# Spreading a closed expert's eight penalties over ScalarE's queue, and starting the first expert on halves of 256 columns

## The chip, the cores and the metric

One core of one Trainium2 chip runs the whole program. The metric is the device time of one execution in microseconds (us); several executions give a median. The engines are TensorE (PE in the rows; PEld is its loading of weights), VectorE (DVE), ScalarE (ACT), GpSimd (POOL) and SyncE (SP). Each takes the instructions of its own queue in the order in which the program put them there.

## The reference

The input is filtered by an FFT along its sequence, and the result goes through eight experts, each with a fixed capacity. Which token goes to which expert is settled by a greedy walk over all scores, highest first:

```python
y = np.fft.irfft(np.fft.rfft(x, axis=1) * F, n=x.shape[1], axis=1)   # 8 x 2496 x 256
x = y.reshape(19968, 256); cap = 19968 // 8                          # 2496 tokens each
logits = x @ w_gate
for idx in np.argsort(-logits.flatten()):
    tok, e = idx // 8, idx % 8
    if assigned[tok] >= 0 or counts[e] >= cap: continue
    assigned[tok] = e; counts[e] += 1
for e in range(8):
    m = assigned == e
    out[m] = np.maximum(x[m] @ w1[e], 0.0) @ w2[e]                   # w1 256x1024, w2 1024x256
```

## The kernel before

**Stages.** The class `Fft` computes the filter and the scores `lg`, and stores the filtered rows to the DRAM tensor `xs`. The class `Route` finds the experts in the order in which they fill up: phase `ph` finds the expert that closes next, its threshold and its members. The class `Ffn` runs that expert. The FFT's last stores of `xs`, the routing of expert 0 and the load of its weights meet at one place, called the handover here.

**One expert.** `Ffn.gather` fetches tokens from `xs` by an index list `xid`, 128 to a tile `xg`, one indirect DMA on POOL's queue each. The 2496 tokens make five groups `g` of 512 (the last of 448), each of four tiles. `Ffn.turn(e, g, h)` turns half a group, two tiles, on PE (`ptr`), then ACT copies it as the rounded high part into a tile named `xo`, and DVE writes the rest into a tile named `z` (the names are those of older tiles whose space is used again). A block `f` of the first product is six matmuls `pz<-xo,w0h`, `pz<-z,w0h`, `pz<-xo,w0l`, three for each half of the 256 inputs, over the 512 columns of a group; eight blocks make the 1024 hidden values. ACT's relu copy (`hl<-pz`, L867) and a DVE instruction (L869) then write the block's high and low part. The second product (`py`, L904) sums 24 matmuls of 256 columns, ACT copies its result (`y`) and POOL scatters it to `out`.

**Weights.** `W.load(0)` and `W.load(1)` fetch the first and second weight of an expert, 1 MiB each, into `wr`. `Ffn.split` cuts each into high and low parts in four pieces: ACT writes `w0h` or `w1h`, DVE writes `w0l` or `w1l`.

**Routing.** `Route.places` lists an expert's members in five chunks of 512; a chunk is one group's index list. For a chunk, DVE makes `GE`, PE runs four matmuls (`rt<-dt,GE`, L772), ACT four sign passes (`junka`, L776), and DVE a few small instructions, of which one writes the chunk's part of `xid` (L781). `Route.phase` also works for the next expert: a maximum `M` over `lg`, masks `tmp`, counts. When expert `vc` is closed, eight ACT instructions (L732), one for each column of `lg`, add a penalty to its column, so that no token picks it again. They stand behind the yield `'w'`.

**What sets the order.** PE's order from the handover on is written out by hand: `manual_schedule` keeps the order in which the code issues its matmuls. All other engines are ordered by a scheduler with a simulated clock. `tc.issue_after(ins)` puts the instructions of its block behind `ins`, but only on the engine of `ins`. `Pump.feed` is called with each yield of `Ffn.run` and lets routing steps go when they are due; `Pump.until` runs them at once until a chunk is made. The call `hook(('g', n))` issues the gather of group `n`.

**The handover in code.** Before the hand-made order begins, `emit` splits the first weight, gathers group 0, loads the second weight and turns both halves of group 0; then it splits the second weight behind the last of these turns:

```python
for h in range(2):
    R.last = W.turn(0, 0, h)
with tc.issue_after(R.last):
    while split:
        W.split(*split.pop(0))
```

`Ffn.run` then begins with `hook(('g', 1))`, so that the places of chunk 1 and the gather of group 1 are issued ahead of the first block.

Of the kernel before, what the change touches and what calls it, by code (L numbers as in the profile page):

```python
# [7 lines left out]
F32, F32R = mybir.dt.float32, mybir.dt.float32r  # L8
BF, F16, I32 = mybir.dt.bfloat16, mybir.dt.float16, mybir.dt.int32
AF, OP, AX = mybir.ActivationFunctionType, mybir.AluOpType, mybir.AxisListType  # L10
# [7 lines left out]
CAP = N  # L18
# [5 lines left out]
TU0, TU, PACE = 1.1, 1.15, 5  # L24
# [108 lines left out]
class Fft:  # L133


    def __init__(s, tc, i, xs, zd, lg, pp):
        s.tc, s.nc, s.i, s.xs, s.zd, s.lg, s.pp = tc, tc.nc, i, xs, zd, lg, pp
        s.zw = s.zo = s.y7 = s.y9 = None
        s.xos = []
        s.nload = s.nstore = 0  # L140
        s.st_x = tc.nc.sync
        s.cps = tc.nc.vector.tensor_copy, tc.nc.scalar.copy
        s.y1c = {}
        s.Y1, s.yt, s.yd, s.z, s.xr, s.vs = {}, {}, {}, {}, {}, {}
# [330 lines left out]
class Route:  # L475
# [5 lines left out]

    def __init__(s, tc, i, lg, cp, wp, ps):
        s.tc, s.nc, s.i, s.lg, s.cp, s.wp, s.ps = tc, tc.nc, i, lg, cp, wp, ps
        s.wb = s.low = None

    def setup(s):
        nc, i = s.nc, s.i
# [154 lines left out]
    def phase(s, ph):  # L642

        nc = s.nc
        v = lambda n, sh, dt=F32, bufs=2: s.wb.tile(sh, dt, name=n, bufs=bufs)

        if 0 < ph < 7:
# [10 lines left out]
            n = s.n = 8 - ph  # L658
# [15 lines left out]
        if ph < 7:  # L674
            n = s.n
            T = s.T

            w, P, c, q, r1 = v("w", [128, 8]), v("P", [128, 16 * n]), v("c", [128, 2 * n]), v("q", [128, 8]), v("r1", [128, 10])
            nc.vector.tensor_tensor(w, s.fw[:, 0:8], s.fw[:, 1:9], op=OP.subtract)
            a = s.c[:, 0:1, 0:1]  # L680
# [15 lines left out]
            x = nc.vector.tensor_copy(tb, tot[:, :2])  # L696
            with s.tc.issue_after(x.ins):
                expert()
                nc.vector.tensor_tensor_scan(cum, s.one[:117], eqm, 0.0, op0=OP.mult, op1=OP.add)
                pen = v("pen", [128, 8])  # L700
# [20 lines left out]
        x = nc.vector.tensor_tensor_scan(tab[:, :S], s.one[:117], mem, 0.0, op0=OP.mult, op1=OP.add)  # L721
# [7 lines left out]
        if ph == 7:  # L729
            return  # L730
        for e in range(8):
            nc.scalar.activation(s.lg[:, :, e], s.lg[:, :, e], AF.Identity, bias=pen[:117, e:e+1], scale=1.0)  # L732
        with s.tc.issue_after(s.last):
            t, t3 = v("u", [117, S]), v("u2", [117, S])
            nc.vector.scalar_tensor_tensor(s.asg, mem, 50.0, s.asg, op0=OP.mult, op1=OP.add)
# [56 lines left out]
class Ffn:  # L792
# [52 lines left out]
    def run(s, e, pump, hook):  # L845

        nc = s.nc
        ids = pump.out[e]
        out_rows = s.out
        _, ((w1h, w1l), (w2h, w2l)) = s.wt[e]  # L850
        hs = {}

        def first(g, f):
            n = min(512, CAP - 512*g)
            xh, xl = s.xT[e, g]
            p = s.ps.tile([128, 512], F32, name="pz", tag="c", bufs=4)
            m = 0
            for k in range(2):
                sl = slice(1024*k+128*f, 1024*k+128*f+128)
                for w, x in ((w1h, xh), (w1h, xl), (w1l, xh)):  # L860
                    nc.tensor.matmul(p[:, :n], w[:, sl], x[:, k, :n], start=m == 0, stop=m == 5)  # L861
                    m += 1
                yield 0.65 * n / 512
            hl = s.wp.tile([128, 1024], F32R, name="hl", bufs=NH)
            hs.setdefault(g, []).append(hl)
            h, l = (hl[:, 512*k:512*k+512] for k in range(2))
            s.lasta = nc.scalar.activation(h[:, :n], p[:, :n], AF.Relu).ins  # L867
            if g < 4:
                s.R.low = nc.vector.scalar_tensor_tensor(l[:, :n], p[:, :n], 0.0, h[:, :n].bitcast(F32), op0=OP.max, op1=OP.subtract).ins  # L869
            else:  # L870
                for a, b, c in ((384, n, n), (0, 384, 512)):
                    s.R.low = nc.vector.scalar_tensor_tensor(hl[:, c:c+b-a], p[:, a:b], 0.0, h[:, a:b].bitcast(F32), op0=OP.max, op1=OP.subtract).ins  # L872

        def firsts(g, count):
            for f in range(len(hs.get(g, ())), min(8, len(hs.get(g, ())) + count)):
                if g + 1 < 5:
                    if f == TF[0]:
                        s.turn(e, g + 1, 0)
                    if f == TF[1]:
                        s.turn(e, g + 1, 1)  # L880
                        if g + 2 < 5:
                            hook(('g', g + 2))
                yield from first(g, f)

        hook(('g', 1))
        for g in range(5):
            n = min(512, CAP - 512*g)
            yield from firsts(g, 8)
            if g == 4:
                hook('last')  # L890
            if g == 0:
                hook('w2')
            for t in range(4):
                if g < 4:
                    yield from firsts(g + 1, ORD[t])
                w = min(128, n - 128*t)
                p = s.ps.tile([128, D], F32, name="py", tag="b", bufs=2)
                half = w == 64
                hi, lo, both = slice(128*t, 128*t+w), slice(512+128*t, 512+128*t+w), slice(384, 512)
                terms = ((both, w2h), (hi, w2l)) if half else ((hi, w2h), (hi, w2l), (lo, w2h))  # L900
                m = 0
                for f in range(8):
                    for a, b in terms:
                        nc.tensor.matmul(p[:a.stop-a.start], hs[g][f][:, a], b[:, 256*f:256*f+256],  # L904
                                         start=m == 0, stop=m == 8 * len(terms) - 1, skip_group_check=half)
                        m += 1
                    if f in ((3,) if half else (1, 3, 5)):
                        yield 0.65
                y = s.wp.tile([128, D], F32, name="y", bufs=4)
                if half:  # L910
                    nc.scalar.copy(y[:w], p[w:])
                    nc.vector.tensor_tensor(y[:w], p[:w], y[:w], op=OP.add)
                else:
                    s.lasta = nc.scalar.copy(y, p).ins  # L914
                st = nc.gpsimd.indirect_dma_start(  # L915
                    out=out_rows, out_offset=bass.IndirectOffsetOnAxis(ap=ids[1][:w, 4*g+t:4*g+t+1], axis=0),
                    in_=y[:w], in_offset=None)
                for o in s.scat:
                    s.tc.declare_no_dep(st.ins, o.ins, reason="each token has one place")
                s.scat.append(st)  # L920
                if t in (1, 2) and g == 4:
                    hook(t)
                yield 0.65


def emit(tc, i, out):
    nc = tc.nc
    with ExitStack() as st:
# [9 lines left out]
        f = Fft(tc, i, xs, zd, lg.rearrange("p (b g) e -> p b g e", g=G), pp)  # L938
# [5 lines left out]
        R = Route(tc, i, lg, None, None, ps)  # L944
# [15 lines left out]
        W = None  # L960
# [20 lines left out]
        split = []  # L981
# [17 lines left out]
        with tc.manual_schedule(engines={mybir.EngineType.PE}):  # L999
            while (0, 0) not in pump.tags:  # L1000
                pump.feed(0.1)
                c = next(units, None)
# [8 lines left out]
        def gather(e, g):  # L1011
            pump.until((e, g))
            W.gather(e, g, pump.out[e])
# [2 lines left out]
        gather(0, 0)  # L1016
        with tc.issue_after(W.lastg):
            W.load(1)
        for h in range(2):
            R.last = W.turn(0, 0, h)  # L1020
        with tc.issue_after(R.last):
            while split:
                W.split(*split.pop(0))
        n = 0
        def flush(p):
            while split and split[0][1] < p:
                with tc.issue_after(W.lasta):
                    W.split(*split.pop(0))
        with tc.manual_schedule(engines={mybir.EngineType.PE}):
            for e in range(8):  # L1030
                pump.limit = e + 1
                def hook(what):
                    if what == 'w2':
                        flush(8)
                    elif isinstance(what, tuple):
                        gather(e, what[1])
                    elif e < 7:
                        if what == 'last':
                            gather(e + 1, 0)
                            flush(4)  # L1040
                        else:
                            W.turn(e + 1, 0, what - 1)
                for pe in W.run(e, pump, hook):
                    pump.feed(pe)
                    n += 1

                    if split and n % PACE == 0:
                        with tc.issue_after(W.lasta):
                            W.split(*split.pop(0))


class Pump:
# [35 lines left out]
    def first(s):  # L1088

        return any((u[1], 0) not in s.tags for u in s.side)  # L1090
# [44 lines left out]
```

## Time and profile before

| | us |
|---|---|
| median of three runs | 1433.83 |
| lowest and highest run | 1430.25, 1435.2 |
| profiled execution: its own time | 1429.82 |
| profiled execution: span of the trace | 1428.0 |
| TensorE busy in the span | 1380.0 (97%) |
| VectorE, ScalarE, GpSimd busy | 899.9, 681.3, 487.5 |

All times in rows count from the start of the span; 1.82 us of the profiled execution lie outside it. The FFT takes the span's first 412 us or so, the eight experts the rest, about 125 us each. The page's busy time of PE is a sum of modelled ends, so the waits on PE were read beside it, and then the rows of each engine around them.

### The profile page before, as it was taken

The numbers are of one execution on the slowest core, as the hardware profiler recorded it, in microseconds if no ns is written. First come the engines' busy times: TensorE is split into PE (matmuls) and PEld (weight loads), VectorE is DVE, ScalarE is ACT, GpSimd is POOL, SyncE is SP. The second block draws the span as 40 slices with busy tenths as digits, with TensorE's granted clock in tenths as the row PEclk, the third lists the DMA queues.
The fourth block names the chain that finished last, engine by engine and source line by source line (L and its number), as shares of the span: only waits on it lengthen the run. The fifth ranks groups of instructions, "written<-read, shape, count | busy, mean of one in ns | idle before, by whom it ended". The sixth has DMA issues, their size and how long they took to land. (4 is left out here: it accounts for less than half of the span.)

```text
span 1428.0 us, 27263 instructions
## 1 busy us (share of the span) xinstructions
PE 1380.0 (97%) x10338; PEld 1210.5 (85%) x10338; DVE 899.9 (63%) x2568; ACT 681.3 (48%) x1658; POOL 487.5 (34%) x538
## 2 busy tenths in 40 slices
PE   8999999998969999999999999999999999999998
PEld 8898898885437898888888888889898899899988
DVE  6677676776547769668667875876867635423231
ACT  7766766644464346226335533533623635423231
POOL 3433433431024126323422632433424333323212
PEclk9999999999989999999999999999999999999999
DMA  9676675658881022102212212112111321111100
GB/s 358 225 223 174 217 217 140 148 130 233 321 314 61 29 82 72 41 23 96 63 36 80 68 43 78 56 43 90 58 34 51 124 71 51 43 45 51 40 19 29
DMA packets 58124, 152.59 MB, mean 107 GB/s; under 512 B 10889, under 2 KB 32137, under 8 KB 54409
## 3 DMA queue, kind: packets, MB, share of 16 engines
q1 hardware_dynamic: 29200, 68.79, 15.9%
q0 software_dynamic: 18416, 60.37, 12.9%
q10 hardware_dynamic: 10377, 21.68, 4.6%
q8 instruction: 82, 1.34, 0.4%
q14 instruction: 49, 0.40, 0.1%
HBM read 87.16 MB, written 63.70 MB: 106 GB/s over the span
## 5 line engine op out<-in xcount | busy, mean ns | idle before, releaser
L904 PE MATMUL py<-w1h,hl 128*128 128x256 f32 x2496 | 485.7, 287 | 1.0 <-DVE hl L872 0.7
L904 PEld LDWEIGHTS py<-w1h,hl 128*128 128x128 f32 x2496 | 403.0, 191 | 7.3 <-issue 3.2
L904 PE MATMUL py<-w1l,hl 128*128 128x256 f32 (+1 forms) x1280 | 359.5, 283 | 0.0
L915 POOL DMA_INDIRECT out<-y,oid x160 | 169.1, 1057 | 506.7 <-ACT y L914 456.5
L867 ACT ACTIVATE hl<-pz 128x512 fp32r<-128x512 f32 (+1 forms) x320 | 187.4, 588 | 226.7 <-PE pz L861 203.1
L861 PE MATMUL pz<-xo,w0h 128*128 128x512 f32 (+1 forms) x640 | 264.3, 413 | 3.0 <-DVE hl L869 1.5
L869 DVE SCALAR_TENSOR_TENSOR hl<-pz,hl 128x512 fp32r<-128x512 f32 x256 | 175.4, 688 | 144.8 <-ACT hl L867 143.4
L861 PE MATMUL pz<-z,w0h 128*128 128x512 f32 (+1 forms) x640 | 248.7, 389 | 0.0
L861 PE MATMUL pz<-xo,w0l 128*128 128x512 f32 (+1 forms) x640 | 248.6, 388 | 0.0
L904 PEld LDWEIGHTS py<-w1l,hl 128*128 128x128 f32 (+1 forms) x1280 | 241.8, 189 | 1.9
L825 POOL DMA_INDIRECT xg<-xs,xid x160 | 170.4, 1065 | 129.8 <-issue 54.2
L914 ACT COPY y<-py 128x256 f32<-128x256 f32 x152 | 56.6, 372 | 305.8 <-PE py L904 262.6
L861 PEld LDWEIGHTS pz<-xo,w0l 128*128 128x128 f32 x640 | 120.8, 189 | 24.1
L861 PEld LDWEIGHTS pz<-xo,w0h 128*128 128x128 f32 x640 | 121.7, 190 | 21.7 <-DVE hl L869 2.3
L861 PEld LDWEIGHTS pz<-z,w0h 128*128 128x128 f32 x640 | 121.7, 190 | 15.7 <-DVE z L843 0.6
L229 ACT COPY Y<-p 64x240 f32<-64x240 f32 (+1 forms) x302 | 115.3, 382 | 23.4 <-PE p L223 16.9
L249 POOL TENSOR_TENSOR P<-P 128x256 f32<-128x256 f32 x80 | 58.9, 737 | 169.4 <-DVE P L247 169.2
L564 DVE TENSOR_TENSOR Gm<-M,thr 117x1232 bf16<-117x1232 f32 (+2 forms) x80 | 104.4, 1315 | 0.2
L223 PE MATMUL p<-cS,xr 117*128 117x120 f32 x688 | 94.0, 276 | 5.9 <-ACT Y L229 2.8
L223 PEld LDWEIGHTS p<-cS,xr 117*128 117x128 f32 x688 | 85.4, 192 | 10.2 <-ACT Y L229 7.5
L241 PE MATMUL p<-cW,Y 128*128 128x128 f32 x640 | 89.7, 277 | 0.7 <-DVE Q L248 0.7
L241 PEld LDWEIGHTS p<-cW,Y 128*128 128x128 f32 x640 | 80.5, 191 | 6.2 <-issue 3.9
(220 smaller groups left out, 2003.5 us busy)
## 6 DMA issues: line engine op xcount, KB each, us to landing
z<-zd SPq DMA_DIRECT2D x26, 600.0 KB, 7.2
zd<-zt SPq DMA_DIRECT2D x120, 128.0 KB, 2.5
xs<-xo ACTq DMA_DIRECT2D x18, 600.0 KB, 6.5
xr<-x SPq DMA_DIRECT2D x6, 1536.0 KB, 10.7
xr<-x SPq DMA_DIRECT2D x6, 1216.0 KB, 9.2
zd<-zt ACTq DMA_DIRECT2D x40, 128.0 KB, 2.8
xs<-xo SPq DMA_DIRECT2D x8, 600.0 KB, 6.4
xr<-x SPq DMA_DIRECT2D x8, 512.0 KB, 6.3
```

The costliest lines, as they stand in the source:

```text
L223: s.lastmm = nc.tensor.matmul(p[:, q-q0, :120], xv[:, q-24*h], s.cS1, start=True, stop=True).ins
L229: c = (nc.vector.tensor_copy if (t == 5 if b else cp) else nc.scalar.copy)(dst, src)
L241: nc.tensor.matmul(p[:, k], s.Y1[b][:, 4*g+k, dh*128:dh*128+128], s.cW[:, 4*g+k], start=True, stop=True)
L249: nc.gpsimd.tensor_tensor(P[:, :, :64], P[:, :, :64], P[:, :, 64:], op=OP.subtract)
L564: nc.vector.tensor_tensor(Gm[:, s0:s1, :m], s.M[:, s0:s1].unsqueeze(2).to_broadcast([117, s1 - s0, m]), thr[:117].unsqueeze(1).to_broadcas ...
L825: s.lastg = s.nc.gpsimd.indirect_dma_start(out=xg[:n], out_offset=None, in_=s.xs, in_offset=bass.IndirectOffsetOnAxis(ap=ids[0][:n, t:t+1] ...
L861: nc.tensor.matmul(p[:, :n], w[:, sl], x[:, k, :n], start=m == 0, stop=m == 5)
L867: s.lasta = nc.scalar.activation(h[:, :n], p[:, :n], AF.Relu).ins
L869: s.R.low = nc.vector.scalar_tensor_tensor(l[:, :n], p[:, :n], 0.0, h[:, :n].bitcast(F32), op0=OP.max, op1=OP.subtract).ins
L904: nc.tensor.matmul(p[:a.stop-a.start], hs[g][f][:, a], b[:, 256*f:256*f+256], start=m == 0, stop=m == 8 * len(terms) - 1, skip_group_check ...
L914: s.lasta = nc.scalar.copy(y, p).ins
L915: st = nc.gpsimd.indirect_dma_start(out=out_rows, out_offset=bass.IndirectOffsetOnAxis(ap=ids[1][:w, 4*g+t:4*g+t+1], axis=0), in_=y[:w], i ...
```

## The change

It has two parts, independent of each other.

**Penalties.** In phases 1 to 6 each of the eight penalty instructions is put behind the relu copy that was issued last (`s.relu`, kept by `first`), and a yield of 1.0 stands between one and the next, so that `Pump.feed` has to let each go. Phase 0, whose penalties come ahead of any relu copy, stays as it was.

**Halves.** For the first expert, `emit` turns only the first half of group 0. `run` then computes the first three blocks over columns 0 to 255 alone (`products(..., 0, 256)`), turns the second half of group 0 after the second of them, and calls `hook('begun')`, which now holds the split of the second weight. Only then comes `hook(('g', 1))`. The three blocks are finished over columns 256 to 511 when `first` reaches them. The condition `R.relu` only keeps the paced splits from asking for a relu copy that isn't there yet.

```diff
         for e in range(8):
-            nc.scalar.activation(s.lg[:, :, e], s.lg[:, :, e], AF.Identity, bias=pen[:117, e:e+1], scale=1.0)
+            with s.tc.issue_after(s.relu) if s.relu else nullcontext():
+                nc.scalar.activation(s.lg[:, :, e], s.lg[:, :, e], AF.Identity, bias=pen[:117, e:e+1], scale=1.0)
+            if s.relu and e < 7:
+                yield 'd', 1.0
...
-        def first(g, f):
-            n = min(512, CAP - 512*g)
+        def products(p, g, f, a, b):
             xh, xl = s.xT[e, g]
-            p = s.ps.tile([128, 512], F32, name="pz", tag="c", bufs=4)
             m = 0
             for k in range(2):
                 sl = slice(1024*k+128*f, 1024*k+128*f+128)
                 for w, x in ((w1h, xh), (w1h, xl), (w1l, xh)):
-                    nc.tensor.matmul(p[:, :n], w[:, sl], x[:, k, :n], start=m == 0, stop=m == 5)
+                    nc.tensor.matmul(p[:, a:b], w[:, sl], x[:, k, a:b], start=m == 0, stop=m == 5)
                     m += 1
-                yield 0.65 * n / 512
+                yield 0.65 * (b - a) / 512
+
+        half = []
+
+        def first(g, f):
+            n = min(512, CAP - 512*g)
+            if half:
+                p = half.pop(0)
+                yield from products(p, g, f, 256, 512)
+            else:
+                p = s.ps.tile([128, 512], F32, name="pz", tag="c", bufs=4)
+                yield from products(p, g, f, 0, n)
...
-            s.lasta = nc.scalar.activation(h[:, :n], p[:, :n], AF.Relu).ins
+            s.lasta = s.R.relu = nc.scalar.activation(h[:, :n], p[:, :n], AF.Relu).ins
...
+        if e == 0:
+            for f in range(3):
+                half.append(s.ps.tile([128, 512], F32, name="pz", tag="c", bufs=4))
+                yield from products(half[f], 0, f, 0, 256)
+                if f == 1:
+                    s.R.last = s.turn(0, 0, 1)
+                    hook('begun')
         hook(('g', 1))
...
-        for h in range(2):
-            R.last = W.turn(0, 0, h)
-        with tc.issue_after(R.last):
-            while split:
-                W.split(*split.pop(0))
+        R.last = W.turn(0, 0, 0)
...
+                    if what == 'begun':
+                        with tc.issue_after(R.last):
+                            while split:
+                                W.split(*split.pop(0))
+                    elif what == 'w2':
...
-                    if split and n % PACE == 0:
+                    if split and R.relu and n % PACE == 0:
```

**PE at the handover.** Before, the last FFT products (`pv`), the four matmuls of chunk 1 of the places (`rt<-dt,GE`, the two pairs shown) and the eight transposes of group 0 stand in this order:

```order
L403 MATMUL pv<-z,cD 120x256
L772 LDWEIGHTS GE
L772 MATMUL rt<-dt,GE 128x180
...
L403 MATMUL pv<-z,cD 120x512
L772 LDWEIGHTS GE
L772 MATMUL rt<-dt,GE 128x180
...
L403 MATMUL pv<-z,cD 120x512
L839 MATMUL ptr<-id,xg 128x128 x8
L861 MATMUL pz<-xo,w0h 128x512
```

Now, from the same place (of the three half blocks, 18 matmuls, four are shown):

```order
L403 MATMUL pv<-z,cD 120x512
L842 MATMUL ptr<-id,xg 128x128 x4
L862 MATMUL pz<-xo,w0h 128x256
...
L862 MATMUL pz<-xo,w0l 128x256
L842 MATMUL ptr<-id,xg 128x128 x4
L862 MATMUL pz<-xo,w0h 128x256
...
L862 MATMUL pz<-xo,w0l 128x256
L775 LDWEIGHTS GE
L775 MATMUL rt<-dt,GE 128x180
```

All four matmuls of chunk 1 now stand behind the three half blocks, with the second halves of these blocks behind them and the turning of group 1 (`ptr<-id,xg` from group 1's tiles) behind those.

**ACT and DVE at the handover.** `w0h` and `w1h` are the splits of the first and second weight, `xo<-ptr` and `z<-ptr` the two copies of a turned half. ACT before:

```order
L818 CAST w0h<-wr_5208 128x512 x4
L842 CAST xo<-ptr 128x2x256 x2
L818 CAST w1h<-wr_5209 128x512 x4
L867 ACTIVATE hl<-pz 128x512 x3
L842 CAST xo<-ptr 128x2x256
```

ACT now:

```order
L821 CAST w0h<-wr_5208 128x512 x4
L845 CAST xo<-ptr 128x2x256
L821 CAST w1h<-wr_5209 128x512 x4
L845 CAST xo<-ptr 128x2x256
L879 ACTIVATE hl<-pz 128x512 x3
L779 ACTIVATE junka,js<-rt,loc 128x176 x4
```

DVE before, with chunk 1's `xid` as its second row:

```order
L780 TENSOR_SCALAR js<-js 128x4
L781 SCALAR_TENSOR_TENSOR xid<-ex,js 128x4
...
L819 TENSOR_TENSOR w0l<-wr_5208,w0h 128x512 x4
L843 TENSOR_TENSOR z<-ptr,xo 128x2x256 x2
L649 TENSOR_REDUCE M<-lg 117x176
L651 TENSOR_TENSOR tmp<-lg,M 117x1408
L564 TENSOR_TENSOR Gm<-M,ic 117x528
```

DVE now, with chunk 1's `xid` as its last row:

```order
L846 TENSOR_TENSOR z<-ptr,xo 128x2x256 x2
L822 TENSOR_TENSOR w1l<-wr_5209,w1h 128x512 x4
L649 TENSOR_REDUCE M<-lg 117x176
L776 TENSOR_TENSOR loc<-sidx,rt 128x2 x2
L769 TENSOR_SCALAR GE<-iota,BC 117x512
L881 SCALAR_TENSOR_TENSOR hl<-pz,hl 128x512 x3
L651 TENSOR_TENSOR tmp<-lg,M 117x1408
L564 TENSOR_TENSOR Gm<-M,ic 117x528
...
L783 TENSOR_SCALAR js<-js 128x4
L653 TENSOR_TENSOR tmp<-tmp,val 117x1408
L784 SCALAR_TENSOR_TENSOR xid<-ex,js 128x4
```

The second half's copy on ACT moved behind the split of the second weight, and chunk 1's `xid` moved from ahead of the first weight's split to behind all of this. POOL's order did not change: four gathers, the second weight's load, and then the gathers of group 1.

**ACT where the fifth expert to fill is closed.** This is the burst of [rows 8]. Before:

```order
L867 ACTIVATE hl<-pz 128x512 x2
L842 CAST xo<-ptr 128x2x256
L732 ACTIVATE lg<-lg,pen 117x176 x8
L867 ACTIVATE hl<-pz 128x512 x3
L818 CAST w0h<-wr_11418 128x512
```

Now, in that phase:

```order
L733 ACTIVATE lg<-lg,pen 117x176 x2
...
L879 ACTIVATE hl<-pz 128x448
L821 CAST w0h<-wr_11692 128x512
L733 ACTIVATE lg<-lg,pen 117x176
L879 ACTIVATE hl<-pz 128x448
L733 ACTIVATE lg<-lg,pen 117x176
L879 ACTIVATE hl<-pz 128x448
L733 ACTIVATE lg<-lg,pen 117x176
```

The run of eight became one of two and six single ones with other ACT work between; in the other phases the longest run is two, three or four.

## Rows read from the trace of the kernel before

**Rows 1.** The page's busy times: engine, us, share of span, instructions.
```profile
PE 1380.0 (97%) x10338; PEld 1210.5 (85%) x10338; DVE 899.9 (63%) x2568; ACT 681.3 (48%) x1658; POOL 487.5 (34%) x538
```

**Rows 2.** Waits of PE, longest first: us in total, times, longest.
```profile
PE ptr L839 <- DMA xg<-xs,xid: 10.8, 2, 10.4
...
PE rt L758 <- DVE tab L721: 3.0, 1, 3.0
...
PE ptr L839 <- DVE hl L869: 1.4, 1, 1.4
```

**Rows 3.** Timeline of PE at the handover: start, duration, instruction, idle before and releaser.
```profile
422.82 1.67 PE L839 MATMUL ptr<-id,xg 128*128 128x128 f32 x6 [10.44 <-DMA xg<-xs,xid]
424.86 0.69 PE L839 MATMUL ptr<-id,xg 128*128 128x128 f32 x2 [0.37 <-DMA xg<-xs,xid]
426.23 0.79 PE L861 MATMUL pz<-xo,w0h 128*128 128x512 f32 x1 [0.68 <-ACT xo L842]
426.95 0.79 PE L861 MATMUL pz<-z,w0h 128*128 128x512 f32 x1
...
435.30 0.50 PE L861 MATMUL pz<-xo,w0h 128*128 128x512 f32 x1 [1.32 <-DVE hl L869]
```

**Rows 4.** Timeline of ACT at the handover.
```profile
422.44 2.18 ACT L818 CAST w0h<-wr 128x512 fp32r<-128x512 f32 x4 [7.90 <-DMA xg<-xs,xid]
424.52 0.58 ACT L842 CAST xo<-ptr 128x512 fp32r<-128x512 f32 x1
425.59 0.59 ACT L842 CAST xo<-ptr 128x512 fp32r<-128x512 f32 x1 [0.49 <-PE ptr L839]
429.25 2.18 ACT L818 CAST w1h<-wr 128x512 fp32r<-128x512 f32 x4 [3.07 <-DMA wr<-w,widx]
```

**Rows 5.** Timeline of DVE around the handover.
```profile
414.45 0.16 DVE L781 SCALAR_TENSOR_TENSOR xid<-ex,js 128x4 int32<-128x4 f32 x1
...
425.55 1.35 DVE L843 TENSOR_TENSOR z<-ptr,xo 128x512 fp32r<-128x512 f32 x2
426.81 1.61 DVE L649 TENSOR_REDUCE M<-lg 117x176 f32<-117x1408 f32 x1
428.46 1.62 DVE L651 TENSOR_TENSOR tmp<-lg,M 117x1408 f32<-117x1408 f32 x1
430.00 0.70 DVE L564 TENSOR_TENSOR Gm<-M,ic 117x528 bf16<-117x528 f32 x1
430.62 1.89 DVE L819 TENSOR_TENSOR w1l<-wr,w1h 128x512 fp32r<-128x512 f32 x3
...
434.56 1.28 DVE L869 SCALAR_TENSOR_TENSOR hl<-pz,hl 128x512 fp32r<-128x512 f32 x2
...
443.69 0.15 DVE L781 SCALAR_TENSOR_TENSOR xid<-ex,js 128x4 int32<-128x4 f32 x1
```

**Rows 6.** Timeline of POOL around the handover.
```profile
422.16 0.94 POOL L825 DMA_INDIRECT xg<-xs,xid  x1 [0.30 <-issue]
423.41 1.19 POOL L809 DMA_INDIRECT wr<-w,widx  x1 [0.30 <-issue]
424.91 0.94 POOL L825 DMA_INDIRECT xg<-xs,xid  x1 [0.30 <-issue]
...
444.57 0.95 POOL L825 DMA_INDIRECT xg<-xs,xid  x1 [13.66 <-PE rt L772]
```

**Rows 7.** Two stretches: length, busy times, granted clock, DMA share, GB/s.
```profile
426.20:429.20 3.00, 2.97 (x6) 2.11 (x7) 2.96 (x4) 0.00 (x0) 2.39 (x3) 0.50 0.92 371
...
886.00:889.00 3.00, 3.00 (x17) 3.00 (x16) 0.69 (x1) 0.89 (x2) 1.00 (x1) 0.52 0.15 49
```

**Rows 8.** Timeline of ACT at one burst of penalties.
```profile
875.04 4.43 ACT L732 ACTIVATE lg<-lg,pen 117x176 f32<-117x176 f32 x8
879.36 1.55 ACT L867 ACTIVATE hl<-pz 128x512 fp32r<-128x512 f32 x3
```

**Rows 9.** Timeline of DVE behind that burst.
```profile
879.97 0.69 DVE L869 SCALAR_TENSOR_TENSOR hl<-pz,hl 128x512 fp32r<-128x512 f32 x1 [3.98 <-ACT hl L867]
```

**Rows 10.** Timeline of PE behind that burst.
```profile
885.32 0.24 PE L758 MATMUL rt<-tab,tri 117*117 117x180 f16 x1 [3.04 <-DVE tab L721]
```

More of the change, by code (lines that the diff above doesn't have):

```diff
@@ L483, in __init__ @@
         s.tc, s.nc, s.i, s.lg, s.cp, s.wp, s.ps = tc, tc.nc, i, lg, cp, wp, ps
-        s.wb = s.low = None
+        s.wb = s.low = s.relu = None
     def setup(s):
@@ L1032, in hook @@
                 def hook(what):
-                    if what == 'w2':
+                    if what == 'begun':
[3 more added lines that the diff above has]
+                    elif what == 'w2':
                         flush(8)
```

## The prediction

> **What bounds the kernel now.** I read the page's busy times first: TensorE has 97% of the span [rows 1], so the end moves by what TensorE loses or wins, and work on other engines counts only where TensorE waits for it. Next I read the waits of TensorE, longest first [rows 2]. Two kinds of them concern the change. One is the handover: 10.8 us in which the first transposes of expert 0 wait for gathered tokens. The other is behind the penalties: 3.0 us for the table of the places, and 1.4 us for a DVE part of `hl`. Then I read each engine's rows around these places. At the handover the reader is to see a staircase: transposes at 422.82 and 424.86, the first product at 426.23, the second at 426.95 because DVE's `z` comes last, and a block held until 435.30 because DVE is late [rows 3]. ACT stands idle there until the second weight lands, and splits it from 429.25 on [rows 4]. DVE goes through the same stretch with large instructions of the next routing phase [rows 5].
>
> **The penalties.** Eight of them hold ACT from 875.04 to 879.47; the relu copies behind come at 879.36 [rows 8]. DVE has waited 3.98 us for the first of these [rows 9], the table of the places is late by that, and TensorE waits 3.04 us [rows 10]. After this idle time the clock was at its lower level, 1.2 GHz: in the 3 us from 886 the granted clock is 0.52 [rows 7], which costs half of them, 1.5 us. With the 1.4 us [rows 2] the bursts cost 3.0 + 1.5 + 1.4 = 5.9 us. The other bursts left no wait of this length in the list. Spread out, a relu copy stands behind one penalty, about 4.43 / 8 = 0.55 us, or behind a run of up to four, 2.2 us. The work itself is the same 48 instructions, on an engine that is busy 48% of the span [rows 1], so it adds nothing to TensorE. The new yields add no instruction; they let routing start later, and it is the next phase's `M` that waits for the last penalty. The bound on one side is the whole 5.9. On the other, were the table as late once more at its new place, 3.0 + 1.5 would be paid again and only 1.4 won. I take a gain of 5.5, near the whole, because every relu copy of the two bad places loses the run of eight that it stood behind.
>
> **The halves: what they win.** TensorE could start when the first half's copies exist. That copy ended at 425.10 on ACT (424.52 + 0.58) [rows 4] and half of DVE's 1.35 us, from 425.55, at 426.23 [rows 5]. The second product would run at 426.23 and not at 426.95 [rows 3]: 0.7 us. Each of three blocks needs twice as many matmuls of half the width; their time lies inside the wait that follows, so its size is of no weight.
>
> **The halves: what they lose.** The index list of group 1 is made of four matmuls on TensorE, four sign passes on ACT and small steps on DVE. Before, DVE wrote that `xid` at 414.45 [rows 5], while TensorE waited for group 0, and the gather of group 1 went out at 424.91, as soon as POOL's queue let it [rows 6]. Now the four matmuls stand behind the half blocks, and the steps that depend on them stand in DVE's queue behind work that waits in turn for ACT. I follow this chain with the durations of before:
> - ACT begins the split of the second weight when the load has landed, 429.25, and needs 2.18 us [rows 4]. The second half's copy, moved behind it, takes 0.59: 432.0.
> - DVE writes the second half's `z`, half of 1.35, to 432.7. Then come four pieces of `w1l`, at 1.89 / 3 = 0.63 each, to 435.2; `M`, 1.61, to 436.8; three parts of `hl`, at 1.28 / 2 = 0.64 each, to 438.7; `tmp`, 1.62, `Gm`, 0.70, and the second `tmp`, for which I take the first's 1.62, to 442.7; and `xid`, 0.15, to 442.8 [rows 5]. Smaller instructions between these are left out.
> - POOL started a gather 0.73 us after its `xid` was there (443.84 to 444.57) [rows 5, 6]: 443.5. The second gather follows after the 1.25 us that lie between 422.16 and 423.41 [rows 6]: 444.8. From its start to the transposes took 2.70 us (422.16 to 424.86) [rows 3, 6], and these take 0.69: the tiles are turned at 448.2.
>
> TensorE's own order puts this turning ahead of block 3, so block 3 starts at 448.2, where it started at 435.30 [rows 3]. Everything that TensorE could do meanwhile is in front of that point and done: the second halves begin at about 432.7 and are 18 matmuls of half the width, so they end before 437. That is a new wait of some 11 us, and block 3 is 12.9 us later. Behind the waiting transposes stand all further matmuls of the program; behind the waiting gather on POOL stand the other gathers and, later, the scatters, none of which is due earlier.
>
> One step is likely earlier. The second weight's load shared the DMA engines with the gathers of group 1, which now start long after it: four tiles of 128 x 256 x 4 bytes, 0.52 MB, at the 371 GB/s of that stretch [rows 7], are 1.4 us. With these, block 3 is 11.5 us later; I take 12, between the two. A page of the Trainium skill bears on this step, "DMA: Bandwidth & Descriptors", section "Anatomy of one DMA — SWDGE (gpsimd) path": it fits such a transfer with 2.0 us and its bytes over 436 GB/s, which for 1 MiB is an estimate of 4.4 us. By the trace this load, beside the gathers, took 5.84 us from POOL's start to the split; by the page's fit the sum would be lower by 1.4 us, and no run here shows the load alone.
>
> After the new wait the clock falls as it did over the first wait: at the handover it was at 0.50 of full speed [rows 7] for the first products. The price is read from the same group: 3 us at about half speed cost 1.5 after an idle time of 3.04; for one nearly four times as long I put the upper end at twice that, 3. I take 2.
>
> The sum for the halves is 12 + 2 = 14 us lost; the 0.7 won lies ahead of the wait and is lost in it. Bounds: 9, if DVE's queue moves up by 3 us more and the clock costs 1.5; 17.5, if the small steps left out add 1.5 and the clock costs 3.
>
> **Sum.** 14 - 5.5 = 8.5 us slower. Against the profiled execution that is 1429.82 + 8.5 = 1438.3. The profiled execution lies 4 us under the median of the runs shown, within their own spread; the difference is carried to the median: 1433.83 + 8.5 = 1442.3. From the bounds, 9 - 5.9 = +3 and 17.5 - 1.4 = +16.1: 1437 to 1450.
>
> **Rivals.**
> *The gather is not late (faster).* If group 1's tiles have landed when the second halves end, there is no new wait. For that its `xid` would have to exist by about 430, and the point that decides is whether DVE reaches the `loc` and `ex` steps of chunk 1 before the `hl` parts and masks that stand ahead of them. Then the change wins 0.7 at the start, the 1.3 of the held block and 5.9 of the bursts: 1433.8 - 7.9 = 1426. For it speaks that DVE was nearly idle ahead of 422; against it, that the four matmuls it depends on stand behind the half blocks, which can't start before 425. Chance 0.10.
> *The wait is short (no change).* If the second weight lands early enough for ACT to be done by 427, and DVE's masks fall into its waits, the chain is some 5 us shorter: 14 - 6 = 8 lost, 5.9 won, 1436. For it speaks that the first half's work on DVE ends at 426.2 and DVE then has nothing to do until the split; against it, that the order of DVE's queue puts the masks behind. Chance 0.15.
> *Routing comes late (slower still).* Seven more yields in six phases start each next phase later. If a later expert's list or weights are then late at its start, one such wait is priced by the nearest row, 3.0 and 1.5 for the clock [rows 2, 7]; at two experts this adds 9: 1451. Against it speaks that expert 1, whose phase starts as before, shows no wait of this size in the list. Chance 0.07.
>
> **How the numbers follow.** The forecast has 0.68. A measurement of this kernel can tell 0.3%, 4.3 us, from no change. The forecast's own range begins at +3, so about 0.06 of its 0.68 falls within 0.3%. Faster: 0.10. Same: the short wait's 0.15, less a little that is slower, plus 0.06, gives 0.19. Slower: 0.71. The range holds the forecast and part of the short wait: 1434.5 to 1450.
>
> **What would show it.** In the trace after, TensorE's list of waits has a second entry for transposes on gathered tokens, of about 11 us, ahead of block 3 of the first group; chunk 1's `xid` is written at about 441 to 443, not ahead of the weights' split; the second half's copy on ACT comes behind four pieces of the second weight; and the clock is at half after it. The waits for the table and for `hl` in the middle of the span are gone. I am wrong if the gather of group 1 goes out before 435, if the second half's copy comes ahead of the weight's split, or if a penalty run still leaves TensorE waiting 3 us.

## The result, and the profile after

The changed kernel takes 1441.92 us (median of six runs, 1441.42 to 1449.43); the kernel before, run beside it, 1430.2. The ratio is 1.0091 with a 95% interval of 1.0075 to 1.0106: 11 to 15 us slower. Its profiled execution has a span of 1440.3 us, against 1428.0.

The waits of PE after (us in total, times, longest), to be read against [rows 2]:

```profile
PE ptr L842 <- DMA xg<-xs,xid: 23.5, 5, 10.9
...
PE py L923 <- DVE hl L884: 3.5, 2, 3.0
...
PE rt L775 <- DVE ex L780: 1.8, 1, 1.8
```

The wait for gathered tokens is now there twice at nearly 11 us. The 3.0 for the table and the 1.4 for `hl` of [rows 2] are gone, and two others have come. PE's timeline at the handover (start, duration, instruction, idle before and releaser), to be read against [rows 3]:

```profile
421.89 1.09 PE L842 MATMUL ptr<-id,xg 128*128 128x128 f32 x4 [10.71 <-DMA xg<-xs,xid]
424.22 0.58 PE L862 MATMUL pz<-xo,w0h 128*128 128x256 f32 x1 [1.24 <-ACT xo L845]
425.31 0.58 PE L862 MATMUL pz<-z,w0h 128*128 128x256 f32 x1 [0.51 <-DVE z L846]
...
444.10 0.66 PE L842 MATMUL ptr<-id,xg 128*128 128x128 f32 x2 [10.90 <-DMA xg<-xs,xid]
445.31 0.69 PE L842 MATMUL ptr<-id,xg 128*128 128x128 f32 x2 [0.55 <-DMA xg<-xs,xid]
445.65 0.78 PE L862 MATMUL pz<-xo,w0h 128*128 128x512 f32 x1
```

Block 3 begins 23.76 us behind the first transposes, where it was 12.48 (435.30 - 422.82) [rows 3]. What held it is a staircase over three engines, to be read against [rows 4, 5]. ACT in the changed kernel:

```profile
427.50 2.18 ACT L821 CAST w1h<-wr 128x512 fp32r<-128x512 f32 x4 [3.33 <-DMA wr<-w,widx]
429.58 0.57 ACT L845 CAST xo<-ptr 128x512 fp32r<-128x512 f32 x1
```

DVE in the same stretch (small steps left out):

```profile
430.19 0.69 DVE L846 TENSOR_TENSOR z<-ptr,xo 128x512 fp32r<-128x512 f32 x1 [4.93 <-ACT xo L845]
430.80 2.48 DVE L822 TENSOR_TENSOR w1l<-wr,w1h 128x512 fp32r<-128x512 f32 x4
433.20 1.61 DVE L649 TENSOR_REDUCE M<-lg 117x176 f32<-117x1408 f32 x1
...
435.12 1.88 DVE L881 SCALAR_TENSOR_TENSOR hl<-pz,hl 128x512 fp32r<-128x512 f32 x3
436.92 1.61 DVE L651 TENSOR_TENSOR tmp<-lg,M 117x1408 f32<-117x1408 f32 x1
438.45 0.70 DVE L564 TENSOR_TENSOR Gm<-M,ic 117x528 bf16<-117x528 f32 x1
...
439.28 1.61 DVE L653 TENSOR_TENSOR tmp<-tmp,val 117x1408 f32<-117x1408 f32 x1
440.82 0.15 DVE L784 SCALAR_TENSOR_TENSOR xid<-ex,js 128x4 int32<-128x4 f32 x1
```

POOL, which has nothing to issue from 422.99 to 441.24:

```profile
422.04 0.95 POOL L812 DMA_INDIRECT wr<-w,widx  x1 [0.30 <-issue]
441.24 0.95 POOL L828 DMA_INDIRECT xg<-xs,xid  x1 [18.25 <-DVE t L790]
```

DVE is not idle between 430.19 and `xid`, which is the last of these in its queue. Two stretches of 2 us after the wait (length, busy of PE, PEld, DVE, ACT, POOL, granted clock, DMA share, GB/s) show the clock at its lower level until about 448 (0.52 over the first stretch), and at full speed behind it:

```profile
446.00:448.00 2.00, 2.00 (x7) 1.53 (x6) 0.69 (x1) 0.59 (x1) 0.59 (x1) 0.52 0.44 131
448.00:450.00 2.00, 2.00 (x13) 1.51 (x12) 0.77 (x2) 0.86 (x2) 0.00 (x0) 1.00 0.00 0
```

### The profile page after: what moved, and what is told of

Same layout as the page of the kernel before. It is cut to its first block, busy times and chain, and to the rows that moved or that the text cites. A ratio compares the mean times of both kernels' runs of the same rounds, so it can differ in the third digit from the quotient of the medians.

```text
span 1440.3 us, 27304 instructions
## 1 busy us (share of the span) xinstructions
PE 1382.8 (96%) x10356; PEld 1215.3 (84%) x10356; DVE 903.1 (63%) x2568; ACT 680.5 (47%) x1658; POOL 477.9 (33%) x538
## 4 chain that ended last, share of the span: by engine, by line
PE 57%; issue 5%; DVE 4%; ACT 2%; POOL 1%; DMA 0%; POOLq 0%; DVEq 0%; ACTq 0%
PE py L923 26%; PE pz L862 26%; PE ptr L842 2%; PE rt L572 2%; POOL out L934 1%; PE rt L775 1%; DVE hl L884 1%; ACT junka L779 1%; ACT lg L733 0%; ACT hl L879 0%; DVE tmp L651 0%; DVE w1l L822 0%; DMA xg<-xs,xid 0%; DVE Gm L564 0%; DVE M L649 0%
## 5 line engine op out<-in xcount | busy, mean ns | idle before, releaser
L934 POOL DMA_INDIRECT out<-y,oid x160 | 165.7, 1035 | 517.6 <-ACT y L933 485.2
L862 PE MATMUL pz<-xo,w0h 128*128 128x512 f32 (+2 forms) x646 | 264.3, 409 | 1.2 <-ACT xo L845 1.2
L862 PE MATMUL pz<-z,w0h 128*128 128x512 f32 (+2 forms) x646 | 250.2, 387 | 1.8 <-DVE z L846 1.3
L862 PE MATMUL pz<-xo,w0l 128*128 128x512 f32 (+2 forms) x646 | 249.9, 387 | 0.0
L828 POOL DMA_INDIRECT xg<-xs,xid x160 | 164.6, 1029 | 120.4 <-issue 61.3
```

Source lines behind the costliest of these rows:

```text
L828: s.lastg = s.nc.gpsimd.indirect_dma_start(out=xg[:n], out_offset=None, in_=s.xs, in_offset=bass.IndirectOffsetOnAxis(ap=ids[0][:n, t:t+1] ...
L862: nc.tensor.matmul(p[:, a:b], w[:, sl], x[:, k, a:b], start=m == 0, stop=m == 5)
L934: st = nc.gpsimd.indirect_dma_start(out=out_rows, out_offset=bass.IndirectOffsetOnAxis(ap=ids[1][:w, 4*g+t:4*g+t+1], axis=0), in_=y[:w], i ...
```

## The experiments

Three marks of the trace cut each run: T, the first transposes of the handover; B, the start of block 3; E, PE's last end. T itself moves by up to 4 us among runs, by the FFT ahead of it. T to B holds the halves, B to E the penalties and the clock behind B. These two columns are of one profiled execution each. The last column is the timed ratio with its interval, against runs of the kernel before on the same chip.

| kernel | T to B | B to E | ratio |
|---|---|---|---|
| before | 12.48 | 987.06 | 1 |
| changed | 23.76 | 988.92 | 1.0091 (1.0075, 1.0106) |
| e1 penalties alone | 12.40 | 984.76 | 0.9973 (0.9957, 0.9988) |
| e2 halves alone | 24.26 | 988.45 | 1.0074 (1.0053, 1.0095) |
| e3 halves, chunk 1 early | 13.84 | 987.70 | 1.0014 (1.0001, 1.0027) |
| e4 halves, copy first | 23.06 | 985.57 | 1.0073 (1.0049, 1.0097) |
| e12 halves, both | 15.13 | 987.89 | 1.0014 (1.0002, 1.0027) |
| e9 changed, longer yields in phases 1, 5 | 25.07 | 992.95 | 1.0121 (1.0101, 1.0140) |
| e10 penalties alone, same | 12.76 | 991.47 | 1.0054 (1.0037, 1.0071) |
| e11 penalties alone, longer in phase 5 | 12.41 | 979.68 | 0.9955 (0.9938, 0.9973) |

### Each half of the change alone

`e1_pen_alone` is the kernel before with the lines on penalties of the diff, and nothing else of it:

```diff
-            nc.scalar.activation(s.lg[:, :, e], ...
+            with s.tc.issue_after(s.relu) if s.relu else nullcontext():
+                nc.scalar.activation(s.lg[:, :, e], ...
+            if s.relu and e < 7:
+                yield 'd', 1.0
...
-            s.lasta = nc.scalar.activation(h[:, :n], p[:, :n], AF.Relu).ins
+            s.lasta = s.R.relu = nc.scalar.activation(h[:, :n], p[:, :n], AF.Relu).ins
```

> The kernel before with the spread penalties alone. Theory A (the yields only move the collision: the next phase's masks come later and fall on DVE's queue at the ends of the experts): the 3.04 us wait for the table and the 1.4 us wait for hl are gone, but PE has new waits of 2 to 3 us for hl and 1 to 2 us for ex, as in the changed kernel, and the time is 0 to 2 us above before. Rival B (the term of the prediction, a gain of 5.5): 5.5 us below before, and the new waits of the changed kernel come from the halves, by what the new start does to the scheduler.

It is 3.9 us faster (2 to 6). Theory A's place was right and its sum wrong: the bursts' waits are gone, and of the new waits one is here, but the gain outlasts it. By time alone Rival B's 5.5 lies within the interval too; its other half, that the new waits come from the halves, does not hold, since this one stands here without them. DVE at the end of expert 4, where it stands (of the rows left out most are steps of the places):

```profile
1046.16 1.61 DVE L649 TENSOR_REDUCE M<-lg 117x176 f32<-117x1408 f32 x1
...
1048.29 0.68 DVE L822 TENSOR_TENSOR w1l<-wr,w1h 128x512 fp32r<-128x512 f32 x1
...
1049.02 1.61 DVE L651 TENSOR_TENSOR tmp<-lg,M 117x1408 f32<-117x1408 f32 x1
...
1050.63 0.70 DVE L564 TENSOR_TENSOR Gm<-M,ic 117x528 bf16<-117x528 f32 x1
1051.24 0.68 DVE L875 SCALAR_TENSOR_TENSOR hl<-pz,hl 128x64 fp32r<-128x64 f32 x2
```

PE there:

```profile
1051.98 0.79 PE L907 MATMUL py<-w1h,hl 128*128 128x256 f32 x2 [2.94 <-DVE hl L875]
```

The last low part of the expert's last group stands behind `tmp` and `Gm` of phase 6. Before, that phase's `M` ran 35 us earlier:

```profile
1011.65 1.61 DVE L649 TENSOR_REDUCE M<-lg 117x176 f32<-117x1408 f32 x1
```

The yields have moved it to a place where PE's next matmul needs that low part. From 1052 to 1055 the granted clock is 0.50, 1.5 us more.

`e2_halves_alone` has the rest of the diff, with the penalties as before:

```diff
-            with s.tc.issue_after(s.relu) if s.relu else nullcontext():
-                nc.scalar.activation(s.lg[:, :, e], ...
-            if s.relu and e < 7:
-                yield 'd', 1.0
+            nc.scalar.activation(s.lg[:, :, e], ...
```

> The kernel before with the halves alone, the eight penalties in one run. Theory A: the halves carry the whole loss, 11 to 12 us (10.35 by which block 3 came later, and 1 to 1.5 of clock). Rival B (penalties gained their 5.5): the halves cost 17 us. The prediction's own term was 14.

It is 10.6 us slower (8 to 14). That fits Theory A, with the prediction's 14 at the upper end of the interval; Rival B's 17 lies outside. With e1 it makes 6.7 for the sum of the parts, and the two together cost 11 to 15: the two parts of the change are not independent, and the penalties' gain is not there behind the halves.

### Which step makes the halves late

`e3_halves_chunk1_early` is e2 with one line moved:

```diff
+        hook(('g', 1))
         if e == 0:
             for f in range(3):
...
-        hook(('g', 1))
         for g in range(5):
```

> The halves alone, with the call that makes chunk 1 and issues the gather of group 1 moved ahead of the half blocks; the second half's ACT copy still stands behind the split of the second weight. Theory A (the late gather of group 1 is the cause): chunk 1's xid is back at about 413 to 415, the wait of 10.9 us ahead of block 3 is gone, block 3 starts at 434 to 437, and the time is within 2 us of before. Rival C (the half blocks cost by themselves, by twice the matmuls of half the width and the low clock, and by the second half behind the split): 5 to 12 us above before although the gather is early.

DVE writes chunk 1's `xid` 8.7 us ahead of T (424.81), as it did before (8.4 us) [rows 3, 5]:

```profile
416.14 0.16 DVE L781 SCALAR_TENSOR_TENSOR xid<-ex,js 128x4 int32<-128x4 f32 x1
```

POOL of e3 issues the gathers of group 1 right behind the load:

```profile
425.07 0.94 POOL L809 DMA_INDIRECT wr<-w,widx  x1 [0.30 <-DMA xg<-xs,xid]
426.32 0.95 POOL L825 DMA_INDIRECT xg<-xs,xid  x1 [0.30 <-issue]
```

The wait of 10.9 is gone, and T to B falls from 24.26 to 13.84. So of the 11.8 us by which the halves alone delay block 3, 10.4 are the late list. What is left is 2.0 us (0 to 4), at the edge of Theory A's range and below Rival C's. Besides the 1.4 us up to B, the clock has a share in it: from 440 to 443 the granted clock is 0.50, where before it was 1.00 in the 3 us behind B.

`e4_halves_copy_first` is e2 with the split of the second weight ordered behind ACT's copy of the second half (`lastx`, kept by `turn`):

```diff
-                        with tc.issue_after(R.last):
+                        with tc.issue_after(R.last), tc.issue_after(W.lastx):
```

> The halves alone, with the second half's ACT copy put ahead of the split of the second weight, chunk 1 still behind the half blocks. Theory A: chunk 1's xid comes 3 to 5 us sooner than in the halves alone, at 436 to 438, block 3 at 440 to 443, and the time is 5 to 8 us above before: the place of the split is a part of the chain, not all of it. Rival D (the split ahead of the copy is the whole loss): within 2 us of before.

A miss for both theories: T to B falls by 1.2 us only, and the time by nothing that can be told. The copy runs 7.0 us behind T (430.67), in e2 8.3: it has to wait for PE, which turns the second half behind two half blocks at half clock, and by then the weight has landed. `xid` is written at 441.91, 18.3 us behind T, against 19.5 in e2. By these rows the chain is what stands ahead of `xid` on DVE, and ACT's order there is worth about 1 us; no run took an instruction out of DVE's queue.

`e12_halves_early_copy_first_again` has both edits.

> The halves alone with chunk 1 ahead of the half blocks and the second half's copy ahead of the second weight's split, on another chip than the first time, where the engines were held at many places by nothing that the trace names. Theory A: block 3 starts 12.0 to 12.8 us behind the first transposes (before 12.5), the time is within 1.5 us of before. Rival C (the half blocks cost by themselves): 2 us or more above before, as with the copy late.

Theory A's number for B was wrong, 15.13, later than with the copy late. DVE in it:

```profile
429.67 0.69 DVE L843 TENSOR_TENSOR z<-ptr,xo 128x512 fp32r<-128x512 f32 x1 [4.28 <-ACT xo L842]
430.27 1.61 DVE L649 TENSOR_REDUCE M<-lg 117x176 f32<-117x1408 f32 x1
431.80 2.49 DVE L819 TENSOR_TENSOR w1l<-wr,w1h 128x512 fp32r<-128x512 f32 x4
434.21 1.62 DVE L651 TENSOR_TENSOR tmp<-lg,M 117x1408 f32<-117x1408 f32 x1
435.74 0.70 DVE L564 TENSOR_TENSOR Gm<-M,ic 117x528 bf16<-117x528 f32 x1
436.36 1.88 DVE L878 SCALAR_TENSOR_TENSOR hl<-pz,hl 128x512 fp32r<-128x512 f32 x3
```

PE, at B:

```profile
437.10 0.50 PE L859 MATMUL pz<-xo,w0h 128*128 128x512 f32 x1 [3.53 <-DVE hl L878]
```

Before, DVE did `M`, `tmp` and `Gm` ahead of the split while PE was on the first three blocks, and the first `hl` ran at 434.56 [rows 5]. The second half's `z` now comes at 429.67 and DVE is idle for 4.28 us ahead of it; the masks come after. PE pays 3.53 where it paid 1.32 [rows 3]. So Theory A is out by the place of block 3. By time, 2.0 us (0 to 4), Rival C's 2 or more is met at its edge and Theory A's 1.5 is not excluded. In none of the forms tried do the halves win: by these rows they make DVE wait, and what they gain at the start is lost.

### Where the penalties' gain goes

In the changed kernel phase 2's masks have been moved to the end of expert 0 as phase 6's were in e1. DVE there:

```profile
556.79 1.61 DVE L649 TENSOR_REDUCE M<-lg 117x176 f32<-117x1408 f32 x1
...
560.25 1.62 DVE L651 TENSOR_TENSOR tmp<-lg,M 117x1408 f32<-117x1408 f32 x1
561.78 0.70 DVE L564 TENSOR_TENSOR Gm<-M,ic 117x528 bf16<-117x528 f32 x1
562.40 0.22 DVE L884 SCALAR_TENSOR_TENSOR hl<-pz,hl 128x64 fp32r<-128x64 f32 x1
...
562.78 0.55 DVE L884 SCALAR_TENSOR_TENSOR hl<-pz,hl 128x384 fp32r<-128x384 f32 x1
```

PE of the changed kernel, behind it:

```profile
563.38 0.39 PE L923 MATMUL py<-w1h,hl 128*128 128x256 f32 x1 [2.98 <-DVE hl L884]
```

At the same place e1 waits 0.33, since there all low parts come ahead of `tmp`. At 1068.16 another 1.81 follow, again behind `M`, `tmp` and `Gm`. Three runs took these places away by the length of a yield.

`e9_after_masks_past_end` is the changed kernel, and `e10_pen_masks_past_end` is e1, with

```diff
-                yield 'd', 1.0
+                yield 'd', 1.3 if ph in (1, 5) else 1.0
```

> The changed kernel with one number changed: yields of 1.3 instead of 1.0 in phases 1 and 5. In its order the masks of phases 2 and 6 stand behind all low parts of hl of expert 0 and expert 4, and no longer ahead of the last of them; the penalties' runs stay short. Theory A (a mask and Gm ahead of an expert's last low parts is what ate the penalties' gain): the waits of 2.98 us at the end of expert 0 and 1.81 at the end of expert 4 go, with 1 to 1.5 us of clock behind each; 4 to 7 us under the changed kernel, that is 5 to 8 us above before. Rival E (behind the halves the penalties have nothing to win): 11 to 13 us above before, as the changed kernel.

> The spread penalties alone with the same number changed. Theory A: the wait of 2.94 us at the end of expert 4 and about 1.5 us of clock behind it go, so that the penalties win 7 to 8 us against before instead of 3.6. Rival G (the masks only collide with something else, further on): 3 to 4 us under before, as the spread penalties alone.

Both miss, in the same way, 17 and 8 us above before; the rivals' totals don't fit either. The waits at the ends of experts 0 and 4 did go. But by their ratios the two are 4 and 12 us slower than the kernels they were made from (the profiled execution of e10, 1432.43, is the fastest of its runs, whose median is 1437.59, and shows less), and in both a wait of 5.23 us has come at the end of expert 2. ACT of e10 there:

```profile
799.58 3.79 ACT L733 ACTIVATE lg<-lg,pen 117x176 f32<-117x176 f32 x7
803.23 0.43 ACT L779 ACTIVATE junka<-rt,loc 128x176 bf16<-128x176 f32 x1
```

DVE's `xid` of expert 3's first list:

```profile
805.76 0.16 DVE L784 SCALAR_TENSOR_TENSOR xid<-ex,js 128x4 int32<-128x4 f32 x1
```

POOL, where a scatter stands ahead of the gather:

```profile
806.00 0.97 POOL L918 DMA_INDIRECT out<-y,oid  x1 [0.74 <-DVE xid L784]
807.27 1.23 POOL L828 DMA_INDIRECT xg<-xs,xid  x1 [0.30 <-issue]
```

PE, which waits for it:

```profile
810.30 0.69 PE L842 MATMUL ptr<-id,xg 128*128 128x128 f32 x2 [5.23 <-DMA xg<-xs,xid]
```

Seven penalties stand in a run after all, ahead of the sign pass of expert 3's list, and the gather is late. The yields put them at an expert's end, where relu copies are 12 us and more apart, so nothing stands between them; e1 has a run of four at the same place (797.98, 2.32 us) and waits 0.50. That this is why they run together, and that the run is what makes the list late, was read from the order, not tried. Rival G has a part in it as well: PE of e10 waits for `z` at five places, 5.1 us in all, where e1 has one such wait of 0.7.

`e11_pen_phase5_longer` gives phase 5 alone the longer yields, which leaves e1's order as it is up to expert 4:

```diff
-                yield 'd', 1.0
+                yield 'd', 1.3 if ph in (5,) else 1.0
```

> The spread penalties alone, with yields of 1.3 in phase 5 only. Its order is that of the spread penalties alone up to expert 4's end; there the masks of phase 6 now stand behind all low parts of hl, and the runs of penalties are of one or two. Theory A (M, tmp and Gm ahead of the last low parts cost 2.94 us and 1.5 of clock at that place): 7 to 8 us under before, where the spread penalties alone were 3.6 under it. Rival G (what is moved there meets another wait of like size): 2 to 5 us under before.

6.4 us under before (4 to 9), 1423.51 us. That lies between Theory A's 7 to 8 and Rival G's 2 to 5, and the interval reaches into both, so the time does not decide. The place does. DVE of e11 at the end of expert 4:

```profile
1050.01 0.68 DVE L875 SCALAR_TENSOR_TENSOR hl<-pz,hl 128x64 fp32r<-128x64 f32 x2
...
1050.76 1.61 DVE L649 TENSOR_REDUCE M<-lg 117x176 f32<-117x1408 f32 x1
```

PE there:

```profile
1050.74 0.51 PE L907 MATMUL py<-w1h,hl 128*128 128x256 f32 x2 [0.20 <-DVE hl L875]
```

The low parts stand ahead of `M`, the wait is 0.20 where e1 has 2.94, and the granted clock is 1.00 from 1051 to 1054. B to E is 5.1 us shorter than e1's, and behind B PE has no wait above 0.75 us. Ahead of that place nothing was moved: counted from T, the first five `M` lie within 0.1 us of e1's. So Theory A's 4.4 of wait and clock are there in the profile. The ratio is the lowest of all kernels run, but its interval overlaps that of e1.

### A chip that tells nothing apart

Four kernels ran on a chip on which the kernel before takes 1448.2 us. `e5_after_phase1_in_one` is the changed kernel without yields in phase 1, `if s.relu and ph not in (1,) and e < 7:`.

> The changed kernel, but phase 1 lets its eight penalties go without yields between; phases 2 to 6 as changed. In its order the masks M and tmp of phase 2 stand back at three quarters of expert 0's low parts of hl, those of phase 6 at 4.75 instead of 4.92 experts; only phase 4's tmp still stands at an expert's end. Theory A (a mask and Gm ahead of the last low parts of an expert is what eats the penalties' gain): the waits of 2.98 us at the end of expert 0 and of 1.81 us at the end of expert 4 go, with 1 to 2 us of clock, and the time is 4 to 6 us under the changed kernel, 1436 to 1438. Rival E (behind the halves the penalties have nothing to win): the same as the changed kernel, 1441 to 1443.

`e6_pen_phase5_in_one` is e1 without yields in phase 5, `ph not in (5,)` in the same place.

> The spread penalties alone, but phase 5 without yields. In its order the masks of phase 6 stand at 4.75 experts instead of 4.92, and one run of eight penalties is back. Theory A: the wait of 2.94 us at the end of expert 4 and 1.5 us of clock behind it go, 4 us under the spread penalties alone, 1422 to 1423. Rival F (the run of eight is what counts): PE waits again for a table or a low part behind the run in phase 5, and the time is that of the spread penalties alone or more, 1426 to 1429.

`e7_pen_short_yields` is e1 with `yield 'd', 0.4`.

> The spread penalties alone with yields of 0.4 instead of 1.0: runs of one to five between relu copies, and the masks of all phases at 0.71 to 0.79 of an expert instead of at its end. Theory A (it is the place of the masks that costs): no wait above 1 us past block 3, and the whole of the prediction's 5.5 or more is won: 1423 to 1425. Rival F (short runs of penalties are what wins, so runs of five give back): 1426 to 1429.

`e8_halves_early_copy_first` is the kernel that e12 took again.

> The halves alone with chunk 1 ahead of the half blocks and the second half's copy ahead of the second weight's split, both. Theory A (late gather, then late copy, make the whole loss): block 3 12.0 to 12.8 us behind the first transposes, where it was 12.5 before and 13.8 with the copy late; the time is 1429 to 1431, the same as before. Rival C (the half blocks cost by themselves): 1433 or more.

Measured were 1480.96, 1455.0, 1457.4 and 1456.93 us, ratios 1.0235, 1.0046, 1.0070 and 1.0051. Apart from Rival C's open "1433 or more" in e8 no theory's totals fit, and e8's 1.0051 against e12's 1.0014 shows how far the chip moves a ratio. Only places can be read: at the ends where the masks were moved away, e5 has 0.93 in place of 2.98, and e6 1.07 in place of 2.94.

## Why the prediction came out, step by step

- **The time** was forecast as 1442.3, and is 1441.92; the difference was forecast as 8.5, and is 11 to 15. That the time came so close is luck. The kernel before, with three more runs, has a median of 1430.2, 3.6 us under the 1433.83 that the forecast started from, and this hides most of the miss. And the two terms missed in opposite directions: the halves, forecast at 14 lost, cost 10.6 alone, and the penalties, forecast at 5.5 won, win nothing behind them. By the profiled executions: block 3 11.3 us later, 1.1 to 1.2 of clock behind it, 0.7 more that is left over up to E, less 0.9 by which T came sooner, make the 12.3 between the spans.
- **The chain to block 3** held link by link. Its end, 25.4 us behind T (448.2 - 422.82), came at 23.76: the weight landed 0.8 sooner after T, and POOL followed `xid` by 0.27, not 0.73. (The 0.73 was read at a gather that [rows 6] puts down to PE, not to `xid`.) Block 3 is 11.3 us later for a term of 12. One link was put in the wrong light: by e4, ACT's split ahead of the copy is worth about 1 us; DVE's queue is the rest.
- **The load without the gathers** was given 1.4 us, and the runs show no such gain. From POOL's start to the split it took 5.46 (422.04 to 427.50) in the changed kernel and 5.79 in e2, both without the gathers of group 1; beside them it took 5.84 before, 5.61 in e3 and 6.08 in e1. The difference is lost in a spread of about half a us. The Trainium skill, "DMA: Bandwidth & Descriptors", section "Anatomy of one DMA — SWDGE (gpsimd) path", would have it at an estimate of 4.4. The measurements without these gathers stay 1.1 to 1.4 above that; group 0's gathers go out just ahead of the load, so no run shows it alone.
- **The clock** was given 2, with bounds of 1.5 to 3. From 445.65 to about 448 at half it cost 1.1 to 1.2 here, less than the lower bound. In e2 the half clock lasted to 452, some 2.4.
- **The penalties' gain of 5.5** is the step that failed. What it counted did go: 3.04, 1.4 and the clock. But "the new yields add no instruction; they let routing start later" was costed at nothing, with no work named that hides it. Alone the gain is 3.9. In the changed kernel waits of 2.98 and 1.81 come back, with a granted clock of 0.50 for 3 us behind each (from 564 and from 1069.2; 1.5 each, priced as in [rows 7]): 7.8 us, more than the 5.9 at stake. That the masks ahead of the low parts make such a wait is shown at one place, by e11. In the changed kernel it is read from the rows: there e9 took the same two waits away and met others. The rival "routing comes late" had this at two experts and 9 us, with a chance of 0.07. It looked for lists and weights that come late; here it was DVE's masks, ahead of the low parts (2.98) and of a step of a list (1.81). The late list did exist as well, 5.23 us, one small step of the yields further on.

## What to carry to other kernels

When a chain of steps is let go later, cost the place where its large instructions come down, on every in-order queue they stand in, and not only the burst that they leave: at an expert's end a mask of 1.6 us and a `Gm` of 0.7 ahead of the last product's input were worth 3 us of PE and 1.5 of clock. A list that gates a gather wants to be made while the engines wait for something else; moving its call by a few lines of code here cost 10 us up to block 3, and 9 of 1430 in time. Spread work by what it stands between, and look at the resulting order for the stretch in which there is nothing to stand between.

## What the runs showed that was not expected

On the chip of e5 to e8 several engines are held together, at many places, with no releaser that the trace names ("issue" or "remote"), for 1 to 9 us. DVE has seven to ten such holds of over 0.9 us in each of the four traces, and none in those from other chips. One such place in e6, on PE:

```profile
458.62 0.44 PE L572 MATMUL rt<-A,Gm 117*48 117x112 bf16 x3 [1.20 <-issue]
```

ACT of e6 at the same time:

```profile
459.41 0.37 ACT L917 COPY y<-py 128x256 f32<-128x256 f32 x1 [8.18 <-remote]
```

And DVE of e6:

```profile
459.50 0.16 DVE L776 TENSOR_TENSOR loc<-sidx,rt 128x2 f32<-128x2 f32 x1 [8.49 <-remote]
```

The same kernel takes 1029.5 us from T to E in e8, and 1003.0 in e12. So a ratio taken on that chip is no measure of an edit of a few us. What holds the engines there stays open.
